# A change to the first batch of an attention-and-mixer kernel: one wide mask matmul per PSUM bank, pairs of heads per tile, loads ahead of the constants

## The chip, the cores and the metric

The kernel runs on one core of one Trainium2 chip. The metric is the device time of one execution in microseconds (us). The four runs of the changed kernel agree within 0.5 %, but many of its variants scatter by 3 to 5 us between executions. The profile is one execution of the same program taken by the hardware profiler. Its engines are PE (TensorE matmuls), PEld (TensorE weight loads), DVE (VectorE), ACT (ScalarE), POOL (GpSimd) and SP (SyncE). An engine name with a q behind it (SPq, POOLq) is the engine's sequencer. The planner described below gives each engine a program of its own.

## The reference

```python
# q, k, v: (8 batches, 8 heads, 576, 64); s: (8, 8, 576); all float32
scores = scale * q @ k.T
cum    = cumsum(maximum(s, 0))
bias   = -(cum[..., :, None] - cum[..., None, :])
scores = where(causal, -1e9, scores + minimum(bias, 0))
x      = softmax(scores) @ v            # (8, 576, 512), the heads side by side
h      = relu(x^T @ w_tok1) @ w_tok2    # token mixing   576 -> 256 -> 576
u      = x + h^T
out    = u + relu(u @ w_ch1) @ w_ch2    # channel mixing 512 -> 1536 -> 512
```

## The kernel before

The kernel is written as a list of operations with modelled durations. A small planner (`Plan.run`) plays the list through, picks for every operation the engine among its alternatives that could start it first, and so fixes each engine's program before anything runs. The diff doesn't say in which order an engine works; the planner does, from modelled times.

A batch goes through scores, Exp (ACT), a causal mask, the product with the values (AV), division by the sum, token mixing, a transpose of the result u into uT, and channel mixing in two products (the first with `wc1`, the second with `wc2`). The bias becomes a weight per key: the values are multiplied by it before AV. Those "value multiplies" and the masks:

```python
# one multiply per 128 keys; five per batch.  Always on POOL, for batch 0 also allowed on DVE
alts = {"POOL": (*c_pool(512, 0.0019), lambda mul=mul: mul(nc.gpsimd))}
if b == 0:
    alts["DVE"] = (0.76, 0.98, lambda mul=mul: mul(nc.vector))
P.op(alts, reads=[(vf, c), "wT"], writes=[(vp, c)], prio=b * 10 + 5 if b else 0)

# causal mask of batches 1 to 7, on DVE, both inputs in SBUF, after the Exp
nc.vector.tensor_tensor(out=o, in0=o, in1=keep[:, :]..., op=ALU.mult)

# POOL issues all loads of k and q, v of batches 0 and 1, and all weights, in one fixed order ("after")
def load_p(fn, key, us, n=1):
    lastp[0] = P.op({"POOL": (0.68 * n, 0, fn)}, writes=key, prio=1, dma=us, after=lastp[0])

stage_qk(0, 0); stage_qk(0, 1)          # k and q of batch 0   (the constants come first, on POOL)
stage_v(0); load_tok()                  # v of batch 0, w_tok1, w_tok2  (w1, w2)
load_ch1 ... stage_qk(1, 0); stage_v(1); stage_qk(1, 1)   # wc1, batch 1
load_ch2(0); load_ch2(1); load_ch2(2)   # wc2
# SP waits here until wc2 has landed, and only then loads v of later batches (a gate)
last[0] = P.op({"SP": ... dma_start(out=gate[0:1, :], in_=wc2[...])}, reads=[("wc2", 2)], ...)
```

In batch 0 the mask is instead added on TensorE: an identity matmul writes -30000 or 0 (`negm`) into PSUM (the memory to which the matmuls of this kernel write), and the scores accumulate on top.

```python
# cut from quad(): batch 0 splits each key block at the diagonal block
cuts = sorted({a, min(z, a + 128), z}) if b == 0 else [a, z]
for a1, z1 in zip(cuts, cuts[1:]):
    if masked:
        for g in heads:    # identity matmul, 128 wide
            nc.tensor.matmul(out=pss[g // 2].t[:, g % 2, o], lhsT=ident, rhs=negm[:, 0 : z1 - a1], start=True, ...)
    for e in range(2):
        for g in heads:    # scores, 64 or 128 wide
            nc.tensor.matmul(..., rhs=qT.t[rows, a1:z1, e], start=(e == 0 and not masked), stop=(e == 1))
```

Lastly, idle stretches of TensorE that the plan foresees before 95 us are filled with matmuls of zeros (line 947 before, line 1003 after), by which the author means to keep its clock up.

## Time and profile before

Median 314.14 us over 3 runs (313.81 to 315.88).

| what | where read | before |
|---|---|---|
| first k load issued | POOL timeline | 2.56 us |
| first AV on TensorE | TensorE timeline | 20.8 us |
| channel mixing of batch 0, first product starts | TensorE timeline | 32.9 us |
| batch 0, second product starts | TensorE timeline | 47.7 us |
| channel mixing of batch 1 starts | TensorE timeline | 81.1 us |
| channel mixing of batch 3 starts | TensorE timeline | 150.2 us |

The table of stretches of the kernel before. Each line gives start and end, length, then busy us (and count of instructions) of each engine, the granted TensorE clock (1.00 is full), the mean busy share of the DMA engines (as the tool counts it, which can exceed 1), and GB/s:

```profile
core 0: us, PE busy (x) PEld busy (x) DVE busy (x) ACT busy (x) POOL busy (x), PEclk, DMA share, GB/s
...
15.00:20.00 5.00, 4.84 (x83) 3.03 (x81) 2.04 (x3) 3.51 (x4) 3.54 (x6) 1.00 1.33 194
...
40.00:50.00 10.00, 8.65 (x107) 6.91 (x107) 8.99 (x18) 5.41 (x12) 4.87 (x6) 1.00 1.18 210
...
70.00:80.00 10.00, 3.69 (x50) 2.45 (x50) 9.97 (x14) 2.91 (x5) 6.91 (x8) 0.76 1.13 248
...
90.00:200.00 110.00, 107.77 (x960) 59.58 (x970) 72.29 (x161) 65.87 (x104) 24.76 (x36) 1.00 0.58 111
```

From 90 us on TensorE is busy 98 % of the time. The time to be won lies before that: in 70 to 80 us TensorE works only 3.69 of 10 us, and its granted clock is 0.76 there, against 1.00 in 60 to 70 us. The DVE timeline of the kernel before shows why (columns: start, length, engine, line, operation, output and inputs). A 128-wide mask, 0.21 us elsewhere, lasts 4.03 us, and a 512-wide one, 0.41 us elsewhere, lasts 3.50 us:

```profile
67.23 4.03 DVE L655 TENSOR_TENSOR E<-E,keep 128x128 bf16<-128x128 bf16 x1
...
74.87 3.50 DVE L647 TENSOR_TENSOR E<-E,keep 128x512 bf16<-128x512 bf16 x1
```

The POOL timeline of the same kernel shows value multiplies at just those times (about 1.04 us each):

```profile
67.51 1.05 POOL L546 TENSOR_TENSOR vp<-vf,wT 128x512 bf16<-128x512 f32 x1
...
74.04 5.23 POOL L546 TENSOR_TENSOR vp<-vf,wT 128x512 bf16<-128x512 f32 x5
```

And the TensorE timeline shows what it costs: two holes (in brackets, with the engine waited for), of which the second ends with the second mask.

```profile
73.47 0.38 PE L763 MATMUL pmx<-h,w 128*128 128x512 bf16 x1 [2.61 <-DVE ub L773]
...
79.02 1.01 PE L799 MATMUL pmx<-ident,ub 128*128 128x128 bf16 x8 [3.58 <-DVE ub L773]
```

The weight loads on POOL stand in one queue:

```profile
11.09 2.59 POOL L699 DMA_DIRECT2D w<-in_moe_w_tok_dram  x4
14.03 0.71 POOL L699 DMA_DIRECT2D wc<-in_moe_w_ch_dram  x1 [0.35 <-DMA vf<-in_v_dram]
15.23 0.71 POOL L699 DMA_DIRECT2D wc<-in_moe_w_ch_dram  x1 [0.49 <-DMA vf<-in_v_dram]
```

### The profile page before, as it was taken

To read this page: it belongs to the slowest core of one execution; us is meant where nothing else is said; L and a number is where in the kernel's file an instruction comes from. 1 tells how busy PE (TensorE), PEld (TensorE's weight loads), DVE (VectorE), ACT (ScalarE), POOL (GpSimd) and SP (SyncE) were. 2 spreads that over 40 slices of the span, in tenths; PEclk is the share of its full clock that TensorE was granted. 3 is DMA by queue.
4 is the path that set the end of the run, shared out by engine and by line. 5 is a ranking of instruction groups with operands and counts; after the bars stand their busy time and mean duration, and the time that the engine had idled before them with its cause. 6 is when DMAs were issued, how large, how long until landed. Compare 5 with 4: busy or idle time off the path is not lost.

```text
span 315.6 us, 6588 instructions
## 1 busy us (share of the span) xinstructions
PE 291.2 (92%) x2632; PEld 166.1 (53%) x2663; DVE 186.4 (59%) x391; ACT 169.8 (54%) x274; POOL 80.3 (25%) x123
## 2 busy tenths in 40 slices
PE   7989989992999998999999999996999999999991
PEld 3566875541676544454774545553764545447540
DVE  6843596999599678455744857694615534350020
ACT  3453965883499367621684268873773256107400
POOL 8764660197015212500160101740000000000000
PEclk9999999997599999999999999998999999999999
DMA  5999999999945896916421854499002410051032
GB/s 107 224 206 232 200 210 217 198 258 245 193 77 117 161 134 134 216 40 120 98 39 39 132 140 75 97 139 209 0 2 51 117 66 3 35 122 63 1 105 73
DMA packets 58343, 38.65 MB, mean 122 GB/s; under 512 B 44480, under 2 KB 47936, under 8 KB 58304
## 3 DMA queue, kind: packets, MB, share of 16 engines
q0 software_dynamic: 10128, 17.93, 33.6%
q1 hardware_dynamic: 48176, 20.21, 27.2%
q8 instruction: 23, 0.38, 0.5%
q14 instruction: 16, 0.13, 0.1%
HBM read 40.71 MB, written 9.44 MB: 159 GB/s over the span
## 4 chain that ended last, share of the span: by engine, by line
PE 76%; DVE 11%; DMA 5%; issue 3%; POOL 3%; ACT 0%; SPq 0%; POOLq 0%; DVEq 0%
PE pmx L827 28%; PE pmx L845 26%; PE psc L620 6%; PE pmx L742 5%; PE pav L677 5%; PE pmx L763 4%; DMA uTb<-ub 3%; DVE ub L773 2%; DVE E L647 2%; POOL vp L546 2%; DVE qT L591 2%; DVE kT L591 2%; DVE x L689 2%; DMA qkn<-in_k_dram 1%; PE psc L615 1%
## 5 line engine op out<-in xcount | busy, mean ns | idle before, releaser
L639 ACT ACTIVATE E<-psc 128x1024 bf16<-128x1024 f32 x64 | 62.5, 1024 | 36.6 <-PE psc L620 36.4
L827 PEld LDWEIGHTS <-wc 128*128 128x128 bf16 x624 | 59.6, 99 | 37.0 <-issue 6.1
L827 PE MATMUL pmx<-uTb,wc 128*128 128x320 bf16 x384 | 59.4, 309 | 3.3 <-DMA uTb<-ub 3.1
L845 PE MATMUL pmx<-wc,gb 128*128 128x512 bf16 x231 | 54.0, 379 | 0.5 <-issue 0.2
L834 ACT ACTIVATE gb<-pmx 128x320 bf16<-128x320 f32 x74 | 32.2, 439 | 29.3 <-PE pmx L827 24.3
L569 ACT ACTIVATE junk<-qkn 128x1152 bf16<-128x1152 bf16 x32 | 37.4, 1169 | 14.5 <-DMA qkn<-in_k_dram 8.8
L845 PE MATMUL pmx<-wc,ga 128*128 128x512 bf16 x184 | 44.2, 379 | 0.7 <-DVE ub L773 0.2
L827 PE MATMUL pmx<-uTa,wc 128*128 128x512 bf16 (+1 forms) x237 | 44.4, 336 | 0.2
L546 POOL TENSOR_TENSOR vp<-vf,wT 128x512 bf16<-128x512 f32 (+1 forms) x35 | 37.2, 1082 | 7.5 <-issue 5.1
L845 PEld LDWEIGHTS <-gb 128*128 128x128 bf16 x240 | 22.5, 98 | 25.4 <-issue 0.4
L563 POOL DMA_DIRECT2D qkn<-in_k_dram x20 | 11.2, 562 | 94.0 <-DVE gb L836 22.9
L677 PEld LDWEIGHTS <-E 128*128 128x128 bf16 x576 | 25.7, 98 | 13.5 <-issue 3.7
L834 ACT ACTIVATE ga<-pmx 128x512 bf16<-128x512 f32 (+1 forms) x43 | 21.8, 508 | 20.4 <-PE pmx L827 19.7
L647 DVE TENSOR_TENSOR E<-E,keep 128x512 bf16<-128x512 bf16 x56 | 28.4, 511 | 4.4 <-ACT E L639 4.4
L689 DVE TENSOR_TENSOR x<-pav,rc 128x320 bf16<-128x320 f32 x60 | 29.4, 490 | 1.8
L677 PE MATMUL pav<-vp,E 128*128 128x65 bf16 x540 | 26.7, 194 | 3.7 <-DVE x L689 2.4
L845 PEld LDWEIGHTS <-ga 128*128 128x128 bf16 x192 | 17.7, 98 | 19.8 <-issue 0.7
L684 DVE RECIPROCAL rc<-pav 128x5 f32<-128x5 f32 x60 | 11.2, 187 | 28.3 <-PE pav L677 28.0
L620 PE MATMUL psc<-qT,kT 32*128 32x256 bf16 (+3 forms) x704 | 25.4, 246 | 0.5 <-DVE qT L591 0.2
L763 PE MATMUL pmx<-h,w 128*128 128x512 bf16 x77 | 20.7, 380 | 2.7 <-DVE ub L773 2.6
L591 DVE STREAM_TRANSPOSE kT<-qkn 128x576 f32<-128x576 f32 x16 | 20.0, 1251 | 4.8 <-PE psc L620 3.3
L856 DVE TENSOR_TENSOR of<-pmx,us 128x512 f32<-128x512 f32 x4 | 2.8, 692 | 33.0 <-PE pmx L845 25.1
(84 smaller groups left out, 262.6 us busy)
## 6 DMA issues: line engine op xcount, KB each, us to landing
out_dram<-of SPq DMA_DIRECT2D x32, 256.0 KB, 2.8
vf<-in_v_dram SPq DMA_DIRECT2D x24, 256.0 KB, 5.4
qkn<-in_k_dram POOLq DMA_DIRECT2D x20, 288.0 KB, 5.5
qkn<-in_q_dram POOLq DMA_DIRECT2D x20, 288.0 KB, 6.5
vf<-in_v_dram POOLq DMA_DIRECT2D x8, 256.0 KB, 9.9
wc<-in_moe_w_ch_dram POOLq DMA_DIRECT2D x4, 384.0 KB, 8.8
wc<-in_moe_w_ch_dram POOLq DMA_DIRECT2D x3, 512.0 KB, 11.6
out_dram<-of SPq DMA_DIRECT2D x8, 128.0 KB, 2.4
```

The costliest lines, as they stand in the source:

```text
L546: eng.tensor_tensor(out=vp.t[p0 : p0 + n, c, :, 0:D], in0=vf.t[p0 : p0 + n, c, :, :], in1=wT[p0 : p0 + n, cw, b * H : b * H + H].unsqueeze ...
L569: P.op({"ACT": (1.2, 1.6, lambda: nc.scalar.activation(out=junk[:, :], in_=n.t[:, :], func=AF.Square, accum_out=sq[:, col : col + 1]))}, r ...
L591: P.op({"DVE": (1.24, 1.4, lambda n=n, dst=dst: nc.vector.transpose(out=dst.t[:, 0:S, :].rearrange("d t e -> d (t e)").bitcast(FP32).rearr ...
L620: nc.tensor.matmul(out=pss[g // 2].t[:, g % 2, o], lhsT=kT.t[rows, j0 : j0 + 128, e], rhs=qT.t[rows, a1:z1, e], start=(e == 0 and not mask ...
L639: nc.scalar.activation(out=E.t[:, :, gi * 512 : gi * 512 + 512], in_=ps.t[:, :, :], func=AF.Exp, scale=0.125)
L647: nc.vector.tensor_tensor(out=o, in0=o, in1=keep[:, :].unsqueeze(1).unsqueeze(1).to_broadcast([128, 2, 2, 128]), op=ALU.mult)
L677: nc.tensor.matmul(out=o[:, ic, 0 : D + 1], lhsT=E.t[:, hh, d0 : d0 + 128], rhs=vp.t[:, jc, h + hh, 0 : D + 1], start=(jc == j_lo), stop=( ...
L689: nc.vector.tensor_tensor(out=x.t[:, :, (h + hh) * D : (h + hh + 1) * D], in0=o[:, :, 0:D], in1=rc.t[:, :].unsqueeze(2).to_broadcast([128, ...
L763: nc.tensor.matmul(out=pm.t[:, :], lhsT=w2[:, t, w0 : w0 + 128], rhs=h1.t[:, t, :], start=(t == 0), stop=(t == NTC - 1 and b > 0))
L827: nc.tensor.matmul(out=pm.t[:, 0 : e - a], lhsT=wc1[:, m, cc * 128 : cc * 128 + 128], rhs=uT.t[:, m, a:e], start=(m == 0), stop=(m == NMC ...
L834: lambda cc=cc, pm=pm, a=a, e=e: nc.scalar.activation(out=g.t[:, cc, a:e], in_=pm.t[:, 0 : e - a], func=AF.Relu),
L845: nc.tensor.matmul(out=pm.t[:, :], lhsT=g.t[:, cc, c * 128 : c * 128 + 128], rhs=wc2[:, cc, :], start=(cc == 0), stop=(cc == NCC - 1))
```

## The change

The intent is to shorten the head, the stretch before TensorE has dense work: half as many, wider matmuls for the scores of batch 0; more PSUM tiles for them (pairs of `pmx` tiles beside `psc`), so that Exp needn't wait; one AV tile and one division per pair of heads; the first loads ahead of the constants on POOL. Further, the token product of batches 0 and 1 is split by heads, transposes are interleaved with it, and a POOL copy ("m1") is meant to hold back the value multiplies of batch 2 until batch 1's masks are done. The core of the diff, with cuts:

```diff
-    negm = sb("negm", [128, 128], BF16, fast)
+    negm = sb("negm", [128, 512], BF16, fast)
-    P.op({"POOL": (1.3, 1.5, consts)}, writes=["const"], prio=0)
-    P.op({"POOL": ... negm ...}, reads=["const"], writes=["negm"], prio=0)
+    def load_consts():
+        lastp[0] = P.op({"POOL": (1.3, 1.5, consts)}, writes=["const"], prio=0, after=lastp[0])
+        lastp[0] = P.op({"POOL": (0.7, 0.9, negs)}, reads=["const"], writes=["negm"], prio=0, after=lastp[0])
 # ... the copy of wT may now also run on ACT
 # value multiplies: the alternatives of batch 0 (POOL, DVE) are as before
-            P.op(alts, reads=[(vf, c), "wT"], writes=[(vp, c)], prio=b * 10 + 5 if b else 0)
+            P.op(alts, reads=[(vf, c), "wT"] + (["m1"] if b == 2 else []), writes=[(vp, c)], prio=b * 10 + 5 if b else 0)
 # ... scores of batch 0
-            pss = [Buf(r_sc, False) for e in range(2)]
+            pss = [Duo() if b == 0 and (qd * 4 + gi * 2 + e) % 3 == 2 else Solo(r_sc) for e in range(2)]
+                if b == 0:
+                    neg = negm[:, :] if gi else negm[:, 0:256].unsqueeze(1).to_broadcast([128, 2, 256])
+                    for g in heads:
+                        nc.tensor.matmul(out=pss[g // 2].bank(g % 2), lhsT=ident[:, :], rhs=neg, start=True, stop=False)
-                    cuts = sorted({a, min(z, a + 128), z}) if b == 0 else [a, z]
 # ... (the scores of a key block are then one matmul, up to 256 wide)
+        if b == 1 and qd == 1:
+            P.op({"POOL": (0.15, 0.3, lambda: [nc.gpsimd.tensor_copy(out=gate[...], in_=Es[e]...) for e in range(2)])},
+                 reads=[(Es[0], 4), (Es[1], 4)], writes=["m1"], prio=0)
 # ... AV
-        for hh in range(2):
-            pa, rc = Buf(r_mx if b == 0 and hh else r_av, False), Buf(r_rc, False)
+        for hs in ([(0, 1)] if b == 0 else [(0,), (1,)]):
+            pa, rc = Solo(r_sc) if b == 0 else Solo(r_av), Buf(r_rc, False)
 # ... token mixing
-        heads = [(0, 4), (4, 6), (6, H)] if b == 0 else [(0, H)]
+        cuts = [[(0, 4)], [(4, 6), (6, H)]] if b == 0 else [[(0, 4)], [(4, H)]] if b == 1 else [[(0, H)]]
-                 writes=[(pm, 0)], holds=[dst], prio=(rank - TOK, 1))
+                 writes=[(pm, 0)], holds=[dst], prio=(rank - TOK, 1 + 0.1 * c))
 # ... (the transposes get 1.15 + 0.1 * c instead of 2; the output stores 0.5 instead of 0)
     stage_qk(0, 0)
     stage_qk(0, 1)
+    load_consts()
+    weights()
     stage_v(0)
```

## The prediction

> **What bounds the kernel now.** By the table of stretches, TensorE is busy 98% from 81 us to the end at clock about 1.0, with one hole (216 us, 3 us, DMA transpose). The time to be won lies before 81 us: zero-filler matmuls take 10.4 us before 32.8 us and 4.7 us between 60 and 81 us, and in 70 to 80 us TensorE is busy 3.7 us.
>
> By the chain of waits, the head has these links:
> 1. first k load issued at 2.56 us (behind the POOL constants), landing 4.43 us later;
> 2. first scores at 9.86 us, then 11 us of serial score matmuls (eight halves of about 1.4 us) until AV at 20.8 us; Exp takes 1.02 us per half with gaps of 0.36 to 0.5 us, so TensorE bounds this;
> 3. AV and token mixing until channel mixing starts at 32.9 us;
> 4. batch 1: values multiplied on POOL until 43.9 us; first channel product over at 47.4 us, wc2 in at 47 us;
> 5. batch 1's token mixing at 65 us, whose end is stuck: a DVE mask of usually 0.2 to 0.4 us takes 4.03 us at 67.2 us, another 3.50 us at 74.9 us, while POOL multiplies values (1.04 us each). [...] TensorE idles about 6 us, and its clock then reads 0.5 from 76 to 84 us (2 to 3 us more).
>
> **Costs of the change.**
> - Loads ahead of constants: first load 1.8 us earlier, and with it the load stream, saturated (DMA share about 1) up to 85 us. Scores start 1.5 us earlier.
> - Scores of batch 0: half as many matmuls, twice as wide. Mask columns rise from 512 or 640 to 1024 per half: 0.43 us against 0.44 to 0.6. The score part should go from 0.67 to about 0.45 us (estimate from 16 matmuls of 256 in 0.57 us later). A half becomes about 0.95 us, so Exp bounds: 5 x 1.02 + 3 x 1.2 (two Exps for pairs of pmx tiles) = 8.8 us instead of 12. Gain 2.5 to 3 us.
> - AV of a pair in one tile: four DVE steps of about 1.1 us against eight of 0.67 us: 0.8 us.
> - Transposes interleaved: 0.5 us.
> - Sum: channel mixing of batch 0 starts near 28 us.
>
> **How much reaches the end.** wc2 lands only some 2 us earlier, so the second channel product starts near 45 us instead of 47.7: 2 to 3 us kept. Batch 1's token mixing (split by heads) can gain 1 to 2 us more. The gate that holds batch 2's values until batch 1's masks are done aims at link 5, but in the old trace those masks were over by 55.4 us; what collides are batch 2's masks. So I expect the stalls to shrink in part, by chance of the new order: full removal is worth about 9 us with the clock, none 0. I take 4 to 5 us.
>
> **Prediction: 306 us**, 8 in 10 between 299 and 312. Faster by over 2%: 0.64; within 2%: 0.33; slower: 0.03.
>
> **What would show it.** First k load at 0.8 us; first Exp near 9.3; AV near 17.5; channel mixing of batch 0 near 28; second channel product near 45; batch 1's channel mixing near 73 (81 before); longest DVE mask under 2 us; clock in 76 to 84 us above 0.8; the same rate after.
>
> **What would make it wrong.** POOL again locking out masks (about 310); all stalls gone (about 300); the new plan opening a hole later; loads bound by bandwidth, not start.

From 314 us, 2 to 3 us kept, 1 to 2 us of batch 1's token mixing and 4 to 5 us of the stalls come to 304 to 307 us, and the figure put down was 306 us. The sizes are estimates, and the trace of the kernel before carries these:

- 0.43 us for 1024 mask columns: twelve 512-wide channel products in a row took 2.59 us (56.69 us, chain of waits), so two take 0.43 us.
- 0.57 us for 16 scores of 256 columns: the 16 at 49.02 us in the same chain.
- 1.2 us for two Exps of a pair: a 512-wide ACTIVATE out of PSUM took 0.60 us.
- 0.67 us for one AV step on DVE: a reciprocal of 0.16 to 0.20 us and a division of 0.49 us. The 1.1 us for a pair is an estimate from one reciprocal and twice the division.
- "saturated": DMA share 1.13 in 10 to 85 us. "2 to 3 us more" for the half clock: in 76 to 84 us it was 0.50, and TensorE was busy for 4.7 us of these; at full clock that would be some 2.4 us.

## More of the kernel before

The profiled execution spans 315.6 us. It took 317.43 us as a run, some 3 us more than the median, so differences read from its trace come out that much too small at the end.

## The result, and the profile after

The kernel after takes **325.78 us** (median of 4 runs, 325.09 to 326.56), against 314.71 us before (4 runs, 313.81 to 315.88). The ratio is 1.035, with a 95 % interval from 1.0305 to 1.0396: slower by 3.5 %. Ratios here are the mean time of one kernel's fast runs over that of the other's fast runs of the same rounds, so they are not quite the ratio of the medians. A run more than 1.5 % above the fastest of its kernel counts as slow and is left out of the ratio, which befell one or two runs of several variants below; the medians and ranges given are over all runs. All profiles compared are of fast runs, with one exception that is named.

| milestone (us) | before | after | difference |
|---|---|---|---|
| first k load issued | 2.56 | 1.23 | -1.3 |
| first AV | 20.8 | 18.2 | -2.6 |
| batch 0, first channel product starts | 32.9 | 29.8 | -3.1 |
| batch 0, second channel product starts | 47.7 | 53.5 | +5.8 |
| batch 1, channel mixing starts | 81.1 | 87.2 | +6.1 |
| batch 3, channel mixing starts | 150.2 | 158.4 | +8.2 |
| end of the span | 315.6 | 324.0 | +8.4 |

The head did become shorter by 3 us. Between 30 and 53 us this turns into a loss of 5.8 us, another 2 us are lost by 158 us, and from there on these two traces stay level. (`before_v0_pool`, an experiment below, has the very TensorE program of the kernel before and was profiled in a run of 314.98 us. Against its trace the end is 10.9 us later: 5.3 us at the second product, 9.0 at batch 3.) The table of stretches of the kernel after answers where to look (same columns as before):

```profile
15.00:20.00 5.00, 4.85 (x70) 2.82 (x71) 2.27 (x4) 4.16 (x5) 3.44 (x5) 1.00 0.52 70
...
40.00:50.00 10.00, 4.85 (x38) 3.38 (x37) 9.05 (x9) 2.26 (x5) 7.27 (x11) 0.81 1.21 207
...
70.00:80.00 10.00, 7.58 (x61) 4.30 (x61) 9.96 (x14) 3.75 (x6) 7.16 (x9) 0.84 1.07 233
80.00:90.00 10.00, 6.28 (x59) 3.94 (x58) 9.82 (x14) 3.11 (x4) 5.43 (x8) 0.67 1.13 186
```

Two things are new. In 15 to 20 us the DMA engines are at 0.52 and 70 GB/s, where the kernel before had 1.33 and 194 GB/s. And in 40 to 50 us TensorE is busy 4.85 us instead of 8.65. The DMA gap is explained by POOL's timeline after. A value multiply of batch 0, for the last 64 keys, now stands *between* the weight loads, and waits there 2.98 us for its v to land:

```profile
11.71 1.87 POOL L739 DMA_DIRECT2D w<-in_moe_w_tok_dram  x3
16.56 1.14 POOL L554 TENSOR_TENSOR vp<-vf,wT 64x512 bf16<-64x512 f32 x1 [2.98 <-DMA vf<-in_v_dram]
17.65 0.78 POOL L739 DMA_DIRECT2D w<-in_moe_w_tok_dram  x1
18.42 2.87 POOL L739 DMA_DIRECT2D wc<-in_moe_w_ch_dram  x4
```

In the kernel before the planner had given all five of these multiplies to DVE. The change didn't touch their list of engines; it altered the modelled times around them, and the planner's choice tipped. While POOL waits, nothing behind it is issued: the first `wc1` load goes out at 18.42 us instead of 14.03. The load right behind the multiply leaves only at 17.65 us, as the multiply ends.

The chain of waits of the kernel after, followed back from 60 us (columns: start, length, what; "issue" is time with no wait that the profile shows), runs just through that multiply:

```profile
11.03 5.46 DMA vf<-in_v_dram
...
16.56 1.14 POOL vp L554
17.69 0.73 POOL w L739
18.43 0.72 POOL wc L739
19.14 7.07 DMA wc<-in_moe_w_ch_dram
...
26.50 12.71 DMA vf<-in_v_dram
...
42.88 3.05 POOL vp L554 x3
...
46.00 1.12 POOL vp L554
...
47.17 0.21 PE pav L719
```

The late stream brings the values of batch 1 late (their multiplies start at 41.3 us instead of 37.4), and TensorE waits for each of them in turn (five holes of 0.8 to 1.4 us, three of them shown), in front of channel products that stand behind in its program. The TensorE timeline after:

```profile
42.36 0.22 PE L719 MATMUL pav<-vp,E 128*128 128x65 bf16 x2 [1.22 <-POOL vp L554]
43.98 0.22 PE L719 MATMUL pav<-vp,E 128*128 128x65 bf16 x2 [1.40 <-POOL vp L554]
...
47.17 0.21 PE L719 MATMUL pav<-vp,E 128*128 128x65 bf16 x1 [0.97 <-POOL vp L554]
```

After these holes the clock is at 0.51 in 46 to 50 us (1.00 there before), and stays at half until 52.7 us. None of the five holes before it, between 41 and 47 us, was longer than 1.40 us. Later in the same trace, holes of 2.27 us (up to 76.8 us) and 3.08 us (up to 84.7 us) go with a clock of 0.50 in 76.8 to 80.0 and in 83.6 to 90.3 us. How the clock depends on the holes isn't shown beyond that. The weights `wc2` are complete at 50.06 us instead of 47.09, as the SP timelines of the kernel before and of the kernel after show by the gate that waits for them:

```profile
47.09 0.60 SPq L880 DMA_DIRECT2D gate<-wc  x1
```

```profile
50.06 0.60 SPq L936 DMA_DIRECT2D gate<-wc  x1
```

Then the blocked masks. (A mask is called blocked here if it lasts far longer than its usual 0.41 or 0.21 us.) On the DVE timeline after, they didn't shrink. There is one of 5.13 us in batch 1, where the longest near there before was 1.17 us, and one of 5.67 us in batch 2:

```profile
41.08 5.13 DVE L683 TENSOR_TENSOR E<-E,keep 128x512 bf16<-128x512 bf16 x1
...
71.36 3.46 DVE L683 TENSOR_TENSOR E<-E,keep 128x512 bf16<-128x512 bf16 x2
...
78.93 5.67 DVE L683 TENSOR_TENSOR E<-E,keep 128x512 bf16<-128x512 bf16 x1
```

The POOL timeline after, around the last of them, also shows the new "m1" copies. They stand *behind* multiplies of batch 2 and in front of batch 3's, so they cannot hold back what they were made to hold back. The diff explains it: the multiplies of batch 2 register that they read "m1" before any operation writes it, so the planner makes the writer wait for the readers, the reverse of the intent.

```profile
79.03 1.05 POOL L554 TENSOR_TENSOR vp<-vf,wT 64x512 bf16<-64x512 f32 x1
80.03 0.30 POOL L661 COPY gate<-E 1x1 bf16<-1x1 bf16 x2
80.29 5.22 POOL L554 TENSOR_TENSOR vp<-vf,wT 128x512 bf16<-128x512 f32 x5
```

### The profile page after: what moved, and what is told of

It reads as the page before. It is cut to its first block, busy times and chain, and to the rows that moved or that the text cites. A ratio compares the mean times of both kernels' runs of the same rounds, so it can differ in the third digit from the quotient of the medians.

```text
span 324.0 us, 6455 instructions
## 1 busy us (share of the span) xinstructions
PE 294.7 (91%) x2559; PEld 166.3 (51%) x2592; DVE 192.5 (59%) x383; ACT 171.0 (53%) x280; POOL 83.1 (26%) x128
## 3 DMA queue, kind: packets, MB, share of 16 engines
q0 software_dynamic: 10128, 17.93, 33.4%
## 4 chain that ended last, share of the span: by engine, by line
PE 67%; DMA 10%; DVE 8%; POOL 6%; issue 4%; ACT 3%; POOLq 0%; DVEq 0%
PE pmx L899 25%; PE pmx L881 24%; DMA vf<-in_v_dram 6%; PE pmx L791 4%; PE psc L647 4%; PE pav L719 4%; PE pmx L817 3%; DMA uTb<-ub 3%; DMA wc<-in_moe_w_ch_dram 2%; POOL vp L554 2%; ACT E L675 2%; DVE E L683 2%; DVE ub L827 1%; POOL vf L542 1%; DVE kT L621 1%
## 5 line engine op out<-in xcount | busy, mean ns | idle before, releaser
L675 ACT ACTIVATE E<-psc 128x1024 bf16<-128x1024 f32 x62 | 60.5, 1026 | 40.6 <-PE psc L647 40.1
L881 PE MATMUL pmx<-uTb,wc 128*128 128x320 bf16 x384 | 58.2, 306 | 3.1 <-DMA uTb<-ub 3.1
L881 PE MATMUL pmx<-uTa,wc 128*128 128x512 bf16 (+1 forms) x237 | 45.4, 341 | 0.2
L554 POOL TENSOR_TENSOR vp<-vf,wT 128x512 bf16<-128x512 f32 (+1 forms) x36 | 38.3, 1081 | 19.9 <-PE pav L719 11.5
L683 DVE TENSOR_TENSOR E<-E,keep 128x512 bf16<-128x512 bf16 x56 | 35.8, 644 | 4.0 <-ACT E L675 3.8
L888 ACT ACTIVATE ga<-pmx 128x512 bf16<-128x512 f32 (+1 forms) x46 | 23.5, 516 | 26.4 <-PE pmx L881 25.6
L729 DVE TENSOR_TENSOR x<-pav,rc 128x320 bf16<-128x320 f32 x56 | 27.4, 490 | 1.7
L647 PE MATMUL psc<-qT,kT 32*128 32x256 bf16 (+1 forms) x620 | 23.0, 257 | 3.7 <-ACT E L675 2.1
L647 PEld LDWEIGHTS <-kT 32*128 32x128 bf16 x640 | 15.3, 94 | 17.3 <-issue 15.6
```

Source lines behind the costliest of these rows:

```text
L554: eng.tensor_tensor(out=vp.t[p0 : p0 + n, c, :, 0:D], in0=vf.t[p0 : p0 + n, c, :, :], in1=wT[p0 : p0 + n, cw, b * H : b * H + H].unsqueeze ...
L647: nc.tensor.matmul(out=pss[g // 2].bank(g % 2)[:, o], lhsT=kT.t[rows, j0 : j0 + 128, e], rhs=qT.t[rows, a:z, e], start=(e == 0 and b > 0), ...
L675: nc.scalar.activation(out=E.t[:, :, gi * 512 : gi * 512 + 512], in_=ps.t[:, :, :], func=AF.Exp, scale=0.125)
L683: nc.vector.tensor_tensor(out=o, in0=o, in1=keep[:, :].unsqueeze(1).unsqueeze(1).to_broadcast([128, 2, 2, 128]), op=ALU.mult)
L729: nc.vector.tensor_tensor(out=x.t[:, :, h0 * D : (h0 + n) * D].rearrange("p c (e d) -> p e c d", e=n), in0=view()[:, :, :, 0:D], in1=rc.t[ ...
L881: nc.tensor.matmul(out=pm.t[:, 0 : e - a], lhsT=wc1[:, m, cc * 128 : cc * 128 + 128], rhs=uT.t[:, m, a:e], start=(m == 0), stop=(m == NMC ...
```

## The experiments

Four theories were held against each other. **A**: the value multiply that went to POOL starves the load queue (about 4 us by 50 us). **B**: POOL's multiplies lock out DVE's masks in 40 to 87 us, that is, make them last several times as long, more than before. **C**: new PSUM tiles, the split token product or new ranks cost something later. **D**: the change of the head itself (wider matmuls, loads first) is of no use or harmful. All outputs are right.

The planner plays its list anew for each kernel, so the rule from above holds for the experiments too. The plans were rebuilt from the kept kernels and compared engine by engine; where an unintended change of order bears on a reading, that is said.

### Is it the multiply on POOL? `v0_on_dve` and `no_gate`

The edit of `v0_on_dve`, against the kernel after, keeps all five multiplies of batch 0 on DVE:

```diff
             if b == 0:
-                alts["DVE"] = (0.76, 0.98, lambda mul=mul: mul(nc.vector))
+                alts = {"DVE": (0.76, 0.98, lambda mul=mul: mul(nc.vector))}
```

> The kernel after, with the five value multiplies of batch 0 on DVE alone (the planner had put the fifth on POOL, in front of the weight loads, where POOL idles 2.98 us for a v load; DMA share 0.52 in 15 to 20 us). Theory A, a stall of the load stream: DMA share in 15 to 20 us back above 1; first wc1 load issued near 14.5 us instead of 18.4; wc2 complete (gate load on the SP queue) near 46.5 us instead of 50.1; batch 1's multiplies start near 38 us instead of 41.3; time 319 to 322 us. Rival B, DVE masks locked out by POOL multiplies (5.1 us at 41 us and 5.7 us at 79 us) are the whole loss: the time stays within 1 us of 325.8, though the loads come earlier.

Measured: 323.53 us (320.8 to 325.86), ratio to before 1.0218 [1.0174, 1.0261], which lies apart from the 1.035 [1.0305, 1.0396] of the kernel after. The load stream is whole again, as its table of stretches shows:

```profile
15.00:20.00 5.00, 5.00 (x82) 3.18 (x82) 2.60 (x5) 3.80 (x5) 4.09 (x6) 1.00 1.16 175
```

The first `wc1` load leaves at 14.23 us, `wc2` is complete at 45.86 us, the multiplies of batch 1 start at 37.2 us, and the second channel product starts at 49.7 us instead of 53.5. So A is right for 3.8 us at 50 us; of these about 2 (by the medians) to 4 (by the ratios) reach the end. But 2 % are still lost. (With the multiply moved, the planner also changed the order of batch 1's scores, AV and channel products in TensorE's program from 33 us of the plan on. The load stream is not touched by that; the time of the second product can be.)

`no_gate` removes the "m1" copies and the reads of them:

> The kernel after without the gate (the two POOL copies and the key m1). By the order of POOL's program the copies stand behind batch 2's multiplies, so they hold the two E tiles of batch 1 until 80 us. Theory C, the gate works backwards and costs: batch 2's second group of scores moves from 85.9 us to below 78 us, and the time falls by 2 to 3 us, to about 323. Rival: batch 2's attention has slack there, and the time stays within 0.7 us of 325.8.

Measured: 329.11 us (325.3 to 331.1), ratio 1.0394 [1.0317, 1.0471]. The expectation failed in part: the second group of batch 2's scores comes at 79.8 and 87.0 us instead of 85.9 and 91.6, earlier but not below 78, and the kernel is no faster. The gate does work backwards, but it is not the loss.

Both together, `v0_dve_no_gate`:

> Both edits together. If A and C are separate and add up: 316 to 319 us, still not clearly faster than before, because masks locked out by POOL remain (longest DVE mask over 3 us). If only B counts: 325. If the gain of the first 30 us (channel mixing of batch 0 starts 3.1 us earlier than before) then comes through: 311 to 313.

324.4 us (323.5 to 328.9), ratio 1.029 [1.0258, 1.0322]: the same picture, nothing to be had from the gate.

### The multiply put into the kernel before: `before_v0_pool` and `before_v0_pool_early`

If A is the mechanism, the kernel before must slow down when the multiply is moved. First attempt, POOL as the only engine for it, with its place left to the planner:

```diff
-            if b == 0:
-                alts["DVE"] = (0.76, 0.98, lambda mul=mul: mul(nc.vector))
+            if b == 0 and c < NJ - 1:
+                alts = {"DVE": (0.76, 0.98, lambda mul=mul: mul(nc.vector))}
```

> The kernel before with one operation moved: the fifth value multiply of batch 0 forced to POOL, where it stands between the second and the third wc1 load; PE, ACT and SP programs are unchanged. Theory A: POOL waits for the v load until about 17.5 us, the third wc1 load is issued near 18.7 us instead of 16.7, the rest of the load stream is 1.5 to 2 us late, and the time grows by 1.5 to 2.5 us, to about 316.5. Rival B: the loads are limited by bandwidth and have slack, under 0.7 us.

314.89 us (314.5 to 316.5), ratio 1.0012 [0.9975, 1.0049]: a miss. The trace told why: the planner placed it behind two `wc1` loads. Those were in the queue already, and the DMA share in 15 to 20 us stayed at 1.39. So it isn't the multiply on POOL as such; it is its place. The second attempt puts it directly behind the `w1` loads, where the kernel after has it:

```diff
+                if c == NJ - 1:
+                    lastmul.append((alts, [(vf, c), "wT"], [(vp, c)]))
+                    continue
 # in load_tok(), between the loads of w1 and of w2:
+        for alts, rd, wr in lastmul:
+            lastp[0] = P.op(alts, reads=rd, writes=wr, prio=1, after=lastp[0])
```

> The kernel before with batch 0's fifth value multiply forced to POOL directly behind the w1 loads and in front of w2 and all wc1 loads, where the kernel after has it. Theory A: POOL waits for the v load to about 17.5 us with nothing queued behind it, the DMA share in 15 to 20 us drops to about 0.5 (1.33 before), wc2 is complete near 50 us instead of 47.1, batch 1's multiplies start near 41 us, and the time grows by 2.5 to 5 us. Rival: as in before_v0_pool nothing comes through, under 1 us.

Measured: **321.82 us (320.75 to 322.51), ratio 1.018 [1.010, 1.026]**. Its POOL timeline and its table of stretches:

```profile
17.66 1.03 POOL L547 TENSOR_TENSOR vp<-vf,wT 64x512 bf16<-64x512 f32 x1 [4.68 <-DMA vf<-in_v_dram]
```

```profile
15.00:20.00 5.00, 4.84 (x83) 3.04 (x82) 1.38 (x2) 3.50 (x4) 2.34 (x3) 1.00 0.75 81
...
40.00:50.00 10.00, 5.34 (x63) 4.06 (x62) 8.93 (x12) 3.41 (x7) 7.57 (x11) 0.84 1.20 207
```

The other signs of the kernel after follow too: `wc2` complete at 51.73 us, batch 1's multiplies at 43.1 us, a mask of 5.11 us at 42.8 us, the second channel product at 54.9 us, batch 1's channel mixing at 91.0 us. One operation of 1 us, moved from DVE into POOL's queue of loads, costs the kernel before some 6 us and recreates the picture in 40 to 50 us. Theory A is shown, in both directions, for the late loads and the waits at batch 1's values. The size has a reservation: here too the planner changed TensorE's program, from 34 us of the plan on (first, three groups of batch 1's scores and one of its AV moved behind channel products). `before_v0_pool`, in which TensorE's program is the same as before, is no test of the size, since its queue did not starve.

### The masks: `v0_dve_hold` and `before_hold`

The edit makes the multiplies of batches 2 and 3 wait, in POOL's own order, behind five small copies that read batch 1's token result:

```diff
+            if b in (2, 3):
+                held.append(vmul)
 # in tok(), for b == 1:
+            def ug():
+                for c in range(4):
+                    nc.gpsimd.tensor_copy(out=ugate[0:1, c : c + 1], in_=u.t[0:1, c, 0:1])
+                nc.gpsimd.tensor_copy(out=ugate[0:1, 4:5], in_=us.t[0:1, 0, 0:1])
+            gop = P.op({"POOL": (0.5, 0.7, ug)}, reads=[(u, c, 0) for c in range(4)] + [(us, 0, 0), (us, 0, 64)], ...)
+            for vmul in held:
+                vmul.deps.add(gop)
```

In `v0_dve_hold` this is put on `v0_on_dve`, in place of the kernel's own gate:

> The same hold in the kernel after with batch 0's multiplies on DVE and without its own gate. Theory B: masks of 2.3, 1.3 and 5.7 us at 67 to 75 us vanish, batch 1's channel mixing starts at 74 to 78 us instead of 83.2, time 314 to 318 us (v0_on_dve 323.5). Rival: above 322.

Measured: **314.01 us (313.2 to 317.7), ratio 0.9973 [0.9886, 1.006]**, against 1.0218 [1.0174, 1.0261] without the hold: 9.5 us less by the medians, 2.5 % by the ratios, and back at the time of the kernel before. Batch 1's channel mixing starts at 72.5 us instead of 83.2. The nearest kernel by its edit is `v0_dve_no_gate` (1.029), which lacks only the hold. Its table of stretches, DVE timeline and TensorE timeline show TensorE more than half idle in 70 to 80 us, a blocked mask, and the AV of batch 2 that waits for it in front of batch 1's work:

```profile
70.00:80.00 10.00, 4.18 (x44) 2.04 (x42) 9.96 (x11) 4.89 (x6) 7.27 (x8) 0.93 1.12 224
...
75.20 5.42 DVE L679 TENSOR_TENSOR E<-E,keep 128x512 bf16<-128x512 bf16 x1
...
80.67 0.46 PE L715 MATMUL pav<-vp,E 128*128 128x65 bf16 x5 [4.10 <-DVE E L679]
```

In the table of stretches of `v0_dve_hold` TensorE is nearly full and at full clock there:

```profile
70.00:80.00 10.00, 8.79 (x99) 5.74 (x98) 9.52 (x14) 8.08 (x14) 6.38 (x12) 1.00 0.79 153
```

Its DVE timeline shows the masks of batch 2 at their normal 0.41 and 0.21 us while POOL does only a load issue and small copies, and long again as soon as the multiplies run (72.42 and 77.39 us on POOL), now with little in TensorE's way (holes of 1.2 us at 75.6 and 81.6 us):

```profile
70.02 0.41 DVE L683 TENSOR_TENSOR E<-E,keep 128x512 bf16<-128x512 bf16 x1
70.34 0.21 DVE L691 TENSOR_TENSOR E<-E,keep 128x128 bf16<-128x128 bf16 x1
...
77.02 3.71 DVE L683 TENSOR_TENSOR E<-E,keep 128x512 bf16<-128x512 bf16 x1
```

The mask and the multiplies have in common that all their inputs are in SBUF (the memory in which the kernel keeps its tiles). The traces show this:

- The masks take 0.21 and 0.41 us without the multiplies. Beside them, in the kernels before and after, a few keep 0.41 us (205.03 us before, 213.52 us after), some take 0.56 to 1.17 us, and others 3.50 to 5.67 us.
- The mask of 5.67 us in the kernel after lasts through one multiply, two small copies and four of the five multiplies behind these. By the records, in which POOL's times are rough, the mask started first (78.93 us, the multiply at 79.03 us; likewise 41.08 and 41.27 us).
- DVE operations of the kernel before that have one input, or one of two in PSUM, kept their times beside the multiplies: STREAM_TRANSPOSE 1.23 us at 65.82 us (1.25 us at 58.28 us, without), TENSOR_SCALAR from `pmx` 0.41 us at 42.72 us, TENSOR_TENSOR from `pmx` and `ua` 0.69 us at 201.16 us (0.69 us at 55.59 us, without). Three small SCALAR_TENSOR_TENSOR with two SBUF inputs took 1.13 us together at 74.74 us in the kernel after, against 0.28 us at 81.67 us in the kernel before, without multiplies.

So theory B is shown as far as these times go; by what means a multiply lengthens a mask is not shown. Two limits belong to it.

- From batch 0's second product to batch 1's channel mixing `v0_dve_no_gate` takes 32.5 us and `v0_dve_hold` 24.9. These 7.6 us are not of the lock-out alone. The two TensorE programs agree up to 68 us of the plan; from there the hold also puts the AV of batch 2 behind batch 1's token product and transposes, so that a blocked mask no longer stands in front of these.
- The same stretch takes 33.4 us in the kernel before, 33.7 in the kernel after and 33.5 in `v0_on_dve`. So the stall was there before, and didn't grow. Removing it pays for the loss of the changed kernel; it isn't the cause of that loss. The 2 % that `v0_on_dve` loses lie elsewhere: 2.0 us up to the second product (where in this execution a mask of batch 1 is blocked for 3.21 us and TensorE waits 2.1 us for it), and 4.8 us after batch 1's channel mixing has started.

The same hold in the kernel before, `before_hold`:

> The kernel before, with five tiny POOL copies that read the results of batch 1's token mixing put in front of the value multiplies of batches 2 and 3, so that POOL multiplies nothing while DVE masks and adds for that token mixing. Theory B (POOL multiplies lock out DVE masks; 4.03 and 3.50 us in the old trace): no mask over 1.1 us between 55 and 80 us, batch 1's channel mixing starts at 73 to 76 us instead of 81.1, little or no half clock there, time 306 to 310 us. Rival: DVE waits for other reasons, or the held multiplies come back as a wait of batch 2's AV: 314 or more.

320.44 us (316.8 to 321.4), ratio 1.0132 [1.0044, 1.022]: a miss. In the profiled execution, the fastest of the four, batch 1's channel mixing starts at 79.2 us instead of 81.1; the time is lost again between batches 3 and 4 (38.7 us instead of 34.7), for a reason that no run isolated. A mask of 5.32 us at 72.7 us remained: the copies read u, and let go before u was transposed. The multiplies then ran into the last masks that stand ahead of the transposed result in DVE's program. So a hold that ends at the wrong moment only moves the collision.

### Other suspects: `v0_dve_few_fills`, `consts_first`, `v0_dve_old_prio`, `v0_dve_unsplit`

Fewer zero matmuls, on `v0_on_dve` (`WARM = 33.0` instead of 95.0):

> The kernel after with batch 0's multiplies on DVE, and zero-filler matmuls only in the first 33 us of the plan. Theory D (fillers stand in TensorE's program where the plan saw idle time, and run at half clock in front of real work: 2.5 us at 47 us in v0_on_dve): second channel product of batch 0 starts near 48 us instead of 49.7, time lower by 1 to 2 us. Rival: fillers keep the clock up, without them the half clock lasts longer and the time rises by 1 to 4 us.

321.79 us (320.2 to 324.1), ratio 1.0203 [1.0122, 1.0283]. The second channel product starts at 48.8 us instead of 49.7, but both this and the end are within the scatter. The rise of 1 to 4 us that the rival named didn't come. The mean granted clock was 0.951 to 0.971 over the four runs, against 0.963 to 0.972 for `v0_on_dve`; so it isn't shown that zero matmuls keep the clock up.

The constants ahead of the loads again, on the kernel after (`load_consts()` moved in front of the two `stage_qk` calls):

> The kernel after with the constants again in front of the first loads; the plan then keeps batch 0's fifth multiply on DVE, so POOL's program is that of before up to 40 us. Compared with v0_on_dve (323.5), which has the loads first and the same multiply on DVE, this shows what the loads ahead are worth by themselves: if the early loads come through to the end, 325; if their lead is lost by 45 us, 323 to 324. If the early loads themselves are what disturbs (POOL constants slower, AFFINE_SELECT 1.08 us instead of 0.29), 321 or less.

321.78 us (317.8 to 323.5), ratio 1.0155 [1.0053, 1.0256] (one of its four runs, the profiled one, counts as slow and is not in the ratio). The planner then leaves all five multiplies on DVE, unasked: `wc2` is complete at 46.43 us in the profile. So it is the move of the loads that tipped the planner. The end is no later than that of `v0_on_dve`: loads first, with the queue whole, is worth nothing at the end.

The old ranks for the later batches and the output stores, on `v0_on_dve`:

> The kernel after with batch 0's multiplies on DVE, and for batches 2 to 7 the old ranks of the second token product (all chunks alike, in front of the next scores) and of the output stores. POOL's program is unchanged. Theory E (the graded ranks push the last token chunks of later batches behind scores that wait for Exp, and cost 1.9 us between the channel mixing of batches 2 and 3 and 2.5 us between 4 and 5 in v0_on_dve): those two intervals shrink to about 27 and 34 us, time 319 to 321 us against 323.5. Rival: the holes come from elsewhere, time within 1 us of 323.5.

323.95 us (322.6 to 324.9), ratio 1.0215 [1.0143, 1.0287]: nothing. The holes of 1.1 and 0.6 us near 120 us stayed.

The token product of batch 1 whole again, on `v0_on_dve` (`cuts` for `b == 1` back to `[[(0, H)]]`):

> The kernel after with batch 0's multiplies on DVE, and batch 1's first token product in one piece again (two pmx tiles, no score tile taken). Theory F: batch 2's second group of scores comes before batch 1's channel mixing (below 75 us instead of 82 and 88 us), and the time falls by 1.5 to 3 us to about 321. Rival: the lock-out of the masks decides alone, 323 to 325.

319.73 us (318.9 to 320.0), ratio 1.0128 [1.0052, 1.0203]. The size is as expected, about 3 us less than `v0_on_dve`, but not by the way that was expected. The scores of batch 2's second group didn't come early, a mask of 4.74 us at 73.5 us stayed, and batch 1's channel mixing starts at 84.0 us. The gain comes later, from there to batch 2's channel mixing: 38.5 us instead of 42.2, without the holes near 120 us. The two intervals overlap; but all eleven fast runs of `v0_on_dve`, `v0_dve_few_fills` and `v0_dve_old_prio`, which all have the split (320.2 to 324.9 us), lie above all four of this kernel (318.9 to 320.0). So the split probably costs some 3 us here; chip and call differ, so it isn't proof.

Not tested one by one are the wider mask matmuls, the pairs of `pmx` tiles and the AV of a pair in one tile.

### Better holds, and what is left of the head: seven more runs

The hold was moved to the right moment, to the transposed result uT of batch 1 (the copies read `uT` instead of u). In the kernel before this is `before_hold_ut`:

```diff
+                for c in range(NJ):
+                    nc.gpsimd.tensor_copy(out=ugate[0:1, c : c + 1], in_=uT.t[0:1, 0, c * 128 : c * 128 + 1])
+            gop = P.op({"POOL": (0.5, 0.7, ug)}, reads=[(uT, c) for c in range(NJ)], writes=["u1"], prio=0)
```

> The kernel before with POOL's multiplies for batches 2 and 3 held until batch 1's transposed token result is complete (before_hold let go too early: a mask of 5.3 us still stood in front of the copies that channel mixing waits for). Theory B: batch 1's channel mixing starts at 73 to 75 us instead of 81, time 306 to 310 us. Rival: 314 or more, since the held multiplies delay batch 2's attention.

313.25 us (310.95 to 316.4), ratio 0.9925 [0.9832, 1.0018]. There is no mask above 1.1 us between 50 and 95 us, and batch 1's channel mixing starts at 75.4 us instead of 81.1. But a mask of 3.54 us at 97.7 us and a hole of 2.6 us up to 101.7 us appear. Over the runs the ratio keeps some 2.4 us of the 5.7; the profiled execution, the fastest of the four, keeps all (its span is 309.1 us instead of 315.6), so where the other runs lose it isn't in a trace.

The changed kernel with this hold, the multiplies on DVE and the old ranks, once with loads and once with constants first:

> The same candidate with the loads ahead of the constants, as in the kernel after. If the early loads are worth nothing, within 1.5 us of hold_ut_consts; if their 3 us lead comes through once the stalls are gone, 2 to 3 us faster.

> A candidate: the kernel after with constants first, batch 0's multiplies on DVE, old ranks for batches 2 to 7, no own gate, and POOL's multiplies for batches 2 and 3 held until all of batch 1's transposed token result is in SBUF (so no mask stands in front of those copies). If theories B and E both hold: batch 1's channel mixing starts near 70 us, time 305 to 310 us. If only B: 311 to 314.

314.37 us (311.4 to 317.2), ratio 0.9957 [0.9863, 1.0051], and 315.9 us (314.0 to 316.8), ratio 0.9962 [0.9885, 1.004]. Both are at the time of the kernel before, and so is the one like the other.

Holding back the multiplies of every later batch, in both kernels (the changed one with multiplies on DVE and whole token product):

> The kernel before with every batch's POOL multiplies from batch 2 on held behind the token mixing that they collide with (batches 2 and 3 behind batch 1's transposed result, batch b behind batch b-2's token result for the later ones). Theory B: as before_hold_ut up to 95 us, and the mask of 3.5 us at 98 us with its hole of 2.6 us vanishes too: 307 to 310 us. Rival: 313 or more, as the multiplies then delay the AV products.

> The same hold in the kernel after with batch 0's multiplies on DVE, no own gate, and batch 1's token product in one piece. If the change's lead of 3 us at the head survives once the collisions are gone: 2 to 4 us faster than before_hold_all. If it is lost at batch 1's values by 44 us anyway: equal within 1.5 us.

314.97 us (312.6 to 316.0), ratio 0.9966 [0.9875, 1.0057], and 319.47 us (315.9 to 321.0), ratio 1.0132 [1.0045, 1.0219]. Both are misses: the masks collide at other places (4.79 us at 107.9 us; in the second, 3.79 us at 111.1 us and 3.30 us at 175.4 us). The second is slower than the first by 4.5 us, which neither of its expectations had; two of its four runs count as slow.

Last, all three repairs in the changed kernel, side by side with a repeat of `before_hold_ut`, five rounds each:

> The kernel after with three repairs at once: the five value multiplies of batch 0 on DVE alone, the token product of batch 1 whole again, and the multiplies of batches 2 and 3 behind POOL copies that read the transposed token result of batch 1. If the repairs add up (hold about -9 us against v0_on_dve, unsplit about -3 us): about 311 us against about 315 for the kernel before, channel mixing of batch 1 near 73 us, ratio 0.985 to 0.99. If the head lead of 3 us reaches the end once stalls are gone, it is faster than before_hold_ut of the same call. If the head lead is absorbed by the start of batch 1, as runs so far say, the two are within 1.5 us.

> The kernel before_hold_ut unchanged, repeated in the same call for a direct comparison on one chip: 312 to 314 us, ratio 0.99 to 1.00.

315.19 us (311.8 to 317.7), ratio 0.9955 [0.9897, 1.0012], and 314.53 us (311.2 to 316.8), ratio 0.9937 [0.9872, 1.0003]. They are equal within their scatter. So with the loss repaired, the shorter head is worth nothing at the end. The TensorE timeline of `hold_ut_unsplit` shows where it goes:

```profile
41.14 0.22 PE L719 MATMUL pav<-vp,E 128*128 128x65 bf16 x2 [1.23 <-POOL vp L556]
...
44.45 0.22 PE L719 MATMUL pav<-vp,E 128*128 128x65 bf16 x1 [0.85 <-POOL vp L556]
```

TensorE comes some 2 us earlier to the AV of batch 1 (39.7 against 42.0 us before), whose values POOL multiplies until about 44 us as before. It waits for one after another (four holes, 3.8 us together; 1.3 us before), and its clock drops to half for 6.8 us (42.8 to 49.6 us). The milestones of several runs say the same:

| kernel | batch 0, first product starts | second product starts |
|---|---|---|
| before | 32.9 | 47.7 |
| v0_dve_hold | 30.6 | 47.6 |
| after_hold_all | 30.5 | 48.1 |
| v0_on_dve | 29.4 | 49.7 |
| hold_ut_loads | 28.7 | 49.3 |
| hold_ut_unsplit | 29.4 | 50.7 |

A start 2 to 4 us earlier never brought a second product that was earlier by more than 0.1 us. The differences among the changed kernels in this table are partly chance: up to 60 us of the plan `v0_on_dve`, `v0_dve_hold` and `hold_ut_loads` have the same TensorE program, and yet start the second product at 49.7, 47.6 and 49.3 us. In the first a mask of 3.21 us at 39.0 us stops TensorE for 2.1 us and the clock falls to half at 42 us; in the second the mask takes 2.20 us and the clock stays full.

The weights gained nothing either. With the queue whole, `wc2` is complete at 45.9 to 47.3 us in the nine kernels with loads first, and at 46.3 to 47.1 us in five variants of the kernel before (their profiled executions): the end of the load stream didn't follow its start. No version was faster than the kernel before beyond its interval; the nearest, the kernel before with the hold until uT, was 0.6 to 0.8 % faster, with an interval that just includes 1.

## Why the prediction was wrong

It said 306.0 us (299 to 312), and 0.03 for slower; the kernel after took 325.78 us.

- **"wc2 lands only some 2 us earlier ... 2 to 3 us kept."** This step failed most. `wc2` came 3 us later (50.06 against 47.09 us), and the second channel product 5.8 us later, since a value multiply moved into the load queue and waited 2.98 us there. The prediction treated the start of the stream as all that can change in it. It took the placement of old operations as given, though the diff changed the modelled times from which a planner places them. `v0_on_dve` gave 3.8 us of it back at 50 us, and `before_v0_pool_early` produced the loss in the kernel before. Even with the queue whole the 2 us didn't come: `wc2` was complete at 45.9 to 47.3 us. That fits "loads bound by bandwidth, not start", which the prediction named as what would make it wrong; that it is bandwidth was not tested.
- **"Sum: channel mixing of batch 0 starts near 28 us."** Right in mechanism, a bit short in size: 29.8 us, a gain of 3.1 of the 4.9 us. The first k load left at 1.23 us (0.8 predicted), the first Exp started at 10.11 us (9.3), AV at 18.2 us (17.5).
- **The lead was carried too far.** The prediction listed, as link 4, that POOL multiplies batch 1's values until 43.9 us, and still passed on 2 to 3 us. Link 4 is a floor: TensorE came earlier, and waited there with its clock falling (to half for 6.8 us in `hold_ut_unsplit`). Repaired versions with the shorter head and the kernel before with the same hold ended equal (315.19 and 314.53 us).
- **"I expect the stalls to shrink in part ... I take 4 to 5 us."** They didn't shrink: from the second product to batch 1's channel mixing it took 33.7 us, against 33.4 before and 28 predicted (45 to 73 us). The longest mask went from 4.03 to 5.67 us (under 2 predicted), and TensorE's clock was 0.76 in 76 to 84 us (above 0.8 predicted) and 0.50 in 84 to 88 us. The new gate was read as aiming at the wrong masks; that its direction is reversed by the order of registration was overlooked.
- **"POOL again locking out masks"** was named as what would make it wrong, at "about 310". It came true, and it is why the hoped-for 4 to 5 us were missing. It doesn't explain a time above that of the kernel before, which had the same stall; how much the longer masks of batch 1 near 40 us add wasn't isolated.
- **"The same rate after"** was wrong by 2 us (from +6.1 us at batch 1's channel mixing to +8.2 at batch 3's), or by some 5 against the trace of `before_v0_pool`. The 2 us arise between the channel mixing of batches 2 and 3 (29.0 us instead of 27.1). The whole token product of batch 1 left that at 29.0 on `v0_dve_unsplit` and gained in the interval before it; and it gave nothing more once the hold was in place (315.19 us against 314.37 us for `hold_ut_loads`, which has it split). The mechanism of these 2 us stays open.

In sum, the ratios are 1.035 (after), 1.022 (multiply back on DVE) and 0.997 (hold added). Of the loss about 1.3 % belongs to the load queue. The intended gain was absorbed at batch 1's values. The hold's 2.5 % repay a stall that the kernel before has too. The remaining 2 % of the loss are spread over the time up to the second product and the batches after the first; the split token product probably has a part in them, and the rest is open. Open is also why a mask beside the multiplies takes at most 1.17 us in some places and 3.50 to 5.67 us in others. The author guesses that this makes the scatter of 3 to 5 us between runs, but no run isolated it.

By milestones, 8.5 us of the miss of 19.8 us stand at the second channel product (53.5 instead of 45 us) and 14.2 us at batch 1's channel mixing (87.2 instead of 73 us).

## What to carry to other kernels

Where a planner places operations from modelled times, compare each engine's program before and after a change, not the diff, and do the same for every experiment: here a multiply that waited 2.98 us for its data, put into the POOL program that issues the loads, held up every load behind it, and the last weights came 3 us later. A stall that is found in the slower kernel is its cause only if the faster kernel hasn't got it too: compare the same stretch in both. A shorter head is worth only what the next floor lets through; look for the first wait in which a different engine's work ends at a fixed time. In these traces a mask with two SBUF inputs took up to 5.67 us instead of 0.41 us beside POOL's multiplies; so keep such work on POOL away from masks that TensorE waits for. A dependency meant to hold it back must be checked in the trace for its direction and its end.
